# A fused attention and two-expert-layer kernel: Silu written into the product's PSUM bank, a new plan, three later loads

## The chip, the cores and the metric

One core of a Trainium2 chip runs the whole program once. The metric is the device time of one execution in microseconds (us), 815.83 us as the median of three executions of the kernel before (813.26 to 817.79). Engines are named as the profile names them: PE is TensorE (PEld its weight loads), DVE is VectorE, ACT is ScalarE, POOL is GpSimd, SP is SyncE, whose queue issues nearly all transfers.

## The reference

Three stages follow each other. An attention-like recurrence with a decaying state per head, over 4 batches, 8 heads, 768 steps and 48 features; a layer whose hidden value is the largest of three products; a gated layer with Silu.

```python
def _attn_ref(r, k, v, w, u):
    for t in range(S):
        cur = einsum('bhd,bhe->bhde', u * k[t], v[t])
        y[t] = einsum('bhd,bhde->bhe', r[t], state + cur)
        state = w[t][..., None] * state + einsum('bhd,bhe->bhde', k[t], v[t])

x = y as 3072 rows of 384
h = maximum(maximum(x @ w1, x @ w2), x @ w3)        # 768 wide
x = h @ w_out                                       # 384 wide
g = x @ w_gate                                      # 1536 wide
out = (g * (1 / (1 + exp(-g))) * (x @ w_val)) @ w_out2
```

## The kernel before

The tokens are cut into six blocks of 512. The first half of the run does the recurrence in 24 steps (six blocks of four head groups) and, as blocks get ready, the first layer: `up` (three products of each of six hidden tiles, whose maximum DVE takes in `up_out`) and `down`. Every fp32 operand is split into a high and a low part, and a product is three matmuls (`mm3`: high by high, high by low, low by high). `wload` brings the raw weights, DVE turns their words into fp32 (`bits`), ACT and DVE split them (`whigh`, `wlow`). `gather` copies 16 rows of one head group into the tiles of the others by DMA; the head group whose number is last in a block (the third row tile, k = 2) needs no gather in block 0, since PE puts its rows in place (`lend`). `up` of block 0 starts as soon as these parts are there.

The second half (from about 404 us) is the gated layer. It goes through three pairs of blocks (d = 0, 1, 2) and, for each, four units of weights, so twelve units n of about 33 us. A unit computes gate (v = 0) and value (v = 1) by a scheme of fewer products: fifteen operands made of sums of blocks (`y_sum` on POOL, split by `op_high` on ACT and `op_low` on DVE or POOL) are multiplied by fifteen sums of weights (`w_sum` on POOL, split by `w_high` on ACT and `w_low`), 45 matmuls per v in `product`. The partial sums in PSUM are taken out by ACT (`snap`, L978) or added by DVE (`join`, L983 and L985, one operand in PSUM and one in SBUF) and POOL (`mix`, L990 and L993, all in SBUF), which leaves six gate tiles and six value tiles in SBUF. For each of the six k, ACT then applies Silu in place in SBUF (`silu`, L997), DVE multiplies the two SBUF tiles into a PSUM bank (`times`, L1004), ACT copies that bank as the high part (`prod_high`, L1018) and DVE subtracts it for the low part (`prod_low`, L1021). Two PSUM banks serve the six products in turn, one named mm3 and one named pt, so the product of a k waits for `prod_low` of the second product before it. The order of k is PORDER = 5, 2, 1, 3, 0, 4. In the next unit, six projections (`proj`, nine matmuls each, the first three for c = 1, then three for c = 0) stand between the products at places that the table GAPS gives, and DVE adds them to the output (`collect`, L1046); one PSUM bank (po) serves most projections in turn.

Nothing in the program is ordered by hand. Plan.order places all instructions of all engines: each item has an engine, a cost, items it waits for and a due time, and due times are passed back to what comes before. At every step it looks at the items that could start within a window of the earliest start, and for each engine takes the smallest key, due + weight x start - a bonus for an item of the same kind as the last. Items marked port get longer when DVE and POOL both work on SBUF. The result is the program order of each engine, and engines run strictly in that order; only waits on data decide at run time. TUNE holds due times of groups (u0 and u1: the splitting of the weights of units 0 and 1; p0 to p3: the splitting of the projection weights; op: the operands of a new d; gaps: which row of GAPS a unit uses). The tiles raw0 and raw1 take turns for every large load of weight words, in a fixed list of turns (chunks): the words of unit 1, the last raw weights, the words of unit 0, then projection words of units 1 and 2, words of unit 2, projection words of unit 0, and so on. A load waits until the last user of its tile is done.

The rows of GAPS that the change speaks of; a key is (v, step after which the projection stands):

```python
# GAPS[0]
    {(0, 10): 0, (0, 13): 1, (1, 2): 2, (1, 6): 3, (1, 9): 4, (1, 12): 5},
# GAPS[1]
    {(0, 10): 0, (0, 13): 1, (1, 3): 2, (1, 8): 3, (1, 10): 4, (1, 12): 5},
# GAPS[2]
    {(0, 10): 0, (0, 13): 1, (1, 8): 2, (1, 9): 3, (1, 11): 4, (1, 13): 5},
# GAPS[6]
    {(0, 11): 0, (0, 14): 1, (1, 4): 2, (1, 7): 3, (1, 10): 4, (1, 12): 5},
```

Of the kernel before, what the change touches and what calls it, by code (L numbers as in the profile page):

```python
# [30 lines left out]
NPART = 5  # L31
W_LO, W_HI = 0.74, 1.35
TINY = 2.0 ** -14
TUNE = {'soon': 13.15, 'up5': -18.02, 'check': 23.6, 'bits': -8.01, 'u1': 339.54, 'u0': 393.49, 'prep': -25.06, 'xpre': 89.82, 'xgap': 8.15, 'xafter': 20.23, 't': -4.09, 'te': 2.32, 'p1': 405.42, 'p2': 412.78, 'p0': 6.62, 'p3': -14.49, 'slow': (3, 5, 6, 8, 10), 'op': -1.97, 'sums': -12, 'mix5': (0, 3), 'words2': -11.06, 'gaps': (1, 0, 3), 'collect': 1.99, 'v': 3.99}
GAPS = (
# [7 lines left out]
)  # L43

class Plan:  # L50
# [20 lines left out]
    def order(self):  # L71
# [27 lines left out]
        while avail:  # L99
            best = None  # L100
            for t in avail:
                at = max([free.get(t["eng"], 0.0), t["after"]] + [
                    d["end"] + d["lat"] + (t["slack"] if d["eng"] != t["eng"] else 0.0) for d in t["deps"]
                ])
                if t["slot"]:
                    o = held_by.get(count.get(t["slot"], 0) % t["slot"])
                    held = [r for r, part in o["readers"] if part in (None, 0)] if o else []
                    if any(r["start"] is None for r in held):
                        continue
                    at = max([at] + [r["end"] + 0.1 for r in held])  # L110
                t["at"] = at
                if best is None or at < best:
                    best = at
            first = {}
            for t in avail:
                if t.get("at") is not None and t["at"] <= best + 0.3:
                    k = first.get(t["eng"])
                    t["key"] = t["due"] + 15 * t["at"] - self.STAY * (t["kind"] == last.get(t["eng"]))
                    if k is None or t["key"] < k["key"]:
                        first[t["eng"]] = t  # L120
            for t in avail:
# [188 lines left out]
def fused(ctx: ExitStack, tc: tile.TileContext, pk, ub, wt_all, out):  # L310
# [439 lines left out]

    def up(c, f, m):
        ps = pss[c, f, m] = mm([128, NT], "ps")
        for k in range(3):
            mm3(ps, hi[f][:, 3 * m + k, :], lo[f][:, 3 * m + k, :], xh[c, k], xl[c, k], k == 0, k == 2)

    def up_out(c, f, m):
        if m == 0 and c == 0:
# [234 lines left out]
            b = buf[n, v, k]  # L992
            nc.gpsimd.tensor_tensor(b, b, buf[n, v, "u" if k == 3 else "d"], ALU.add)  # L993

    def silu(n, k):
        b = buf[n, 0, k]
        nc.scalar.activation(b, b, AF.Silu)  # L997

    gated = {}

    def times(n, k):
        e = PORDER.index(k) % 2
        gated[n, k] = (psO[0] if e else psM).tile([128, NT], F32, tag="pt" if e else "mm3", name="pt")
        nc.vector.tensor_tensor(gated[n, k], buf[n, 0, k], buf[n, 1, k], ALU.mult)  # L1004

    MIX5 = TUNE["mix5"]
    FINALS = (5, 2, 0, 1, 3, 4)
# [64 lines left out]

    p = Plan()

    SHARED = (y_sum, w_sum, op_low, w_low, mix, times, p_low, hidden, bits)

    def on(eng, cost, fn, *args):
        port = fn in SHARED and eng in ("DVE", "POOL")
# [6 lines left out]
            return t  # L1085
        return make

    UP0, PERIOD, LAST = 33.0, 62.0, 49.0
    START = [UP0 + (PERIOD * c + 6 if c else 0) for c in range(NC_)]
    SECOND = START[5] + LAST  # L1090

# [291 lines left out]
            L["chain"] = before  # L1383


    L["outer", 3]["deps"].append(L["take", 2])
    L["state0", 3]["deps"].append(L["lower", 2])
    L["suffix", 4]["deps"].append(L["state1", 3])
# [106 lines left out]
    def finish(n, k, j, due):  # L1495
        e = PORDER.index(k)
        by = AT_P[n, 0] - 4 + TUNE["te"] * e
        t = L["times", n, k] = on("DVE", 0.62, times, n, k)([j, L["silu", n, k]] + ([L["pl", *last_t[0]]] if len(last_t) > 1 else [L["y1d", 5, q] for q in range(3)]), by + TUNE["t"], slack=0.2)
        last_t[:] = last_t[-1:] + [(n, k)]
        if n == NU - 1:  # L1500
            war = [("x", n, 1, FINALS.index(k))]
        elif n:
            war = [("pj", n - 1, k % 2, 2)]
        else:
            war = [L["down", 5, 2, 1]] + (users[24] if k in (1, 3) else [L["wl", m, v, e] for m in STAGED for v in range(2) for e in range(3)] if k == 2 else [])
        h = on("ACT", 0.6, prod_high, n, k)([t], by - 2, slack=0.3)
        waits.append((h, war))
        slow = False
        L["pl", n, k] = on("POOL" if slow else "DVE", 1.35 if slow else 0.62, prod_low, n, k, nc.gpsimd if slow else nc.vector)([h], by - 1, slack=0.3)

    def buf_war(n, v, k):
        prev_ = (n, 0) if v else (n - 1, 1)
        first_ = [L["down", 5, 2, 1], close]
        if k == "u":
            return [L["mix", *prev_, 3], L["mix", *prev_, 5]] if prev_[0] >= 0 else first_
        if k == "d":
            return [L["mix", *prev_, 4], L["mix", *prev_, 5]] if prev_[0] >= 0 else first_
        pv = n - len(BUFS[v, k])
        if pv < 0:
            return first_  # L1520
        return [L["times", pv, k]]

    STEPS = (("s", 1), ("s", 0), ("s", "u"), ("j", "u"), ("s", 3), ("s", 4), ("s", "d"), ("s", 2), ("j", 2), ("j", 5),
             ("j", 2), ("j", 0), ("j", 1), ("j", 3), ("j", 4))
# [3 lines left out]
    def x_step(n, v, i, due):  # L1528
# [27 lines left out]
            L["mix", n, v, 4] = on("POOL", 1.35, mix, n, v, 4)([a, act[n, v, 5]], due + 4, slack=0.4)  # L1556
        if i in (9, 10, 11, 12, 13, 14):
            if v == 0:
                L["silu", n, k] = on("ACT", 0.6, silu, n, k)([a], due + SOON + 6, slack=0.5)
            else:  # L1560
                ready[k] = a
                if i == 14:
                    for q in PORDER:
                        finish(n, q, ready[q], due + SOON)
# [145 lines left out]
```

## Time and profile before

| what | value |
|---|---|
| device time, median of three (range) | 815.83 us (813.26 to 817.79) |
| the profiled execution's own time | 817.55 us |
| its span, first to last instruction | 815.8 us |
| PE busy | 788.6 us, 97% |
| DVE busy | 643.2 us, 79% |
| ACT busy | 458.2 us, 56% |
| POOL busy | 301.9 us, 37% |
[...]

The profile is of one execution. Busy shares are averages over stages with different limits; what a change is worth is read at the places where PE stands still, and there from what ended the wait.

### The profile page before, as it was taken

The numbers are of one execution on the slowest core, as the hardware profiler recorded it, in microseconds if no ns is written. First come the engines' busy times: TensorE is split into PE (matmuls) and PEld (weight loads), VectorE is DVE, ScalarE is ACT, GpSimd is POOL, SyncE is SP. The second block draws the span as 40 slices with busy tenths as digits, with TensorE's granted clock in tenths as the row PEclk, the third lists the DMA queues.
The fourth block names the chain that finished last, engine by engine and source line by source line (L and its number), as shares of the span: only waits on it lengthen the run. The fifth ranks groups of instructions, "written<-read, shape, count | busy, mean of one in ns | idle before, by whom it ended". The sixth has DMA issues, their size and how long they took to land.

```text
span 815.8 us, 15826 instructions
## 1 busy us (share of the span) xinstructions
PE 788.6 (97%) x6140; PEld 642.9 (79%) x6140; DVE 643.2 (79%) x930; ACT 458.2 (56%) x983; POOL 301.9 (37%) x281
## 2 busy tenths in 40 slices
PE   6999999999999999999999999999999999999997
PEld 5788668888888888888777887768888878888885
DVE  7889999977979967689758769796486787846864
ACT  5633564665454744445368655665864786666340
POOL 1000255221131010279848888533543262212210
PEclk9599999999999999999989999999999999999999
DMA  9745465774675752678683548678786776657202
GB/s 290 217 157 187 139 166 161 211 248 110 182 220 160 195 195 96 226 262 316 238 293 154 189 173 299 226 272 283 245 299 216 264 268 208 238 157 254 95 1 81
DMA packets 46482, 167.02 MB, mean 205 GB/s; under 512 B 6048, under 2 KB 11040, under 8 KB 41152
## 3 DMA queue, kind: packets, MB, share of 16 engines
q1 hardware_dynamic: 46256, 165.81, 62.2%
q8 instruction: 50, 0.82, 0.4%
q14 instruction: 32, 0.26, 0.1%
q10 hardware_dynamic: 144, 0.13, 0.1%
HBM read 123.84 MB, written 40.11 MB: 201 GB/s over the span
## 4 chain that ended last, share of the span: by engine, by line
PE 88%; DVE 6%; ACT 2%; issue 2%; DMA 1%; POOL 1%; SPq 0%; DVEq 0%; ACTq 0%; POOLq 0%
PE px L969 15%; PE py L969 13%; PE ps L660 10%; PE ps L662 10%; PE ps L661 10%; PE po L660 6%; PE po L662 6%; PE po L661 6%; PE y L550 2%; PE ps L781 2%; PE kp L524 2%; DVE W L933 2%; PE sc L606 2%; PE sc L510 1%; PE pa L481 1%
## 5 line engine op out<-in xcount | busy, mean ns | idle before, releaser
L969 PE MATMUL px<-yo,W 128*128 128x512 f32 x567 | 148.7, 394 | 5.8 <-ACT sb L978 3.1
L969 PE MATMUL py<-yo,W 128*128 128x512 f32 x498 | 132.1, 390 | 0.0
L969 PEld LDWEIGHTS px<-yo,W 128*128 128x128 f32 x567 | 107.5, 190 | 30.3 <-DVE sb L983 4.0
L993 POOL TENSOR_TENSOR sb<-sb 128x512 f32<-128x512 f32 x46 | 62.4, 1359 | 182.6 <-ACT sb L978 159.9
L660 PE MATMUL ps<-xh,hi 128*128 128x512 f32 x324 | 129.9, 401 | 0.0
L662 PE MATMUL ps<-xh,lo 128*128 128x512 f32 x324 | 127.2, 393 | 0.0
L661 PE MATMUL ps<-xl,hi 128*128 128x512 f32 x324 | 127.2, 393 | 0.0
L969 PEld LDWEIGHTS py<-yo,W 128*128 128x128 f32 x498 | 93.9, 189 | 19.6
L983 DVE TENSOR_TENSOR sb<-px,sb 128x512 f32<-128x512 f32 x95 | 64.2, 685 | 37.0 <-PE px L969 32.9
L660 PE MATMUL po<-pr,Wp 128*128 128x512 f32 x213 | 83.8, 393 | 3.0 <-DVE acc L1046 3.0
L661 PE MATMUL po<-pr,Wp 128*128 128x512 f32 x213 | 83.1, 390 | 1.3 <-DVE pr L1021 1.3
L662 PE MATMUL po<-pr,Wp 128*128 128x512 f32 x213 | 83.0, 390 | 0.0
L1018 ACT ACTIVATE pr<-pt 128x512 fp32r<-128x512 f32 x71 | 42.0, 599 | 61.2 <-DVE pt L1004 55.9
L978 ACT ACTIVATE sb<-px 128x512 f32<-128x512 f32 x96 | 56.5, 599 | 35.1 <-PE px L969 31.9
L662 PEld LDWEIGHTS ps<-xh,lo 128*128 128x128 f32 x324 | 61.4, 189 | 13.1
L660 PEld LDWEIGHTS ps<-xh,hi 128*128 128x128 f32 x324 | 61.6, 190 | 12.8 <-issue 0.2
L661 PEld LDWEIGHTS ps<-xl,hi 128*128 128x128 f32 x324 | 61.6, 190 | 12.3 <-issue 0.2
L424 POOL COPY total<-I 128x8 f32<-128x8 f32 x24 | 12.3, 514 | 156.3 <-DVE s L442 75.8
L1004 DVE TENSOR_TENSOR pt<-sb 128x512 f32<-128x512 f32 x71 | 63.5, 909 | 0.6
L764 DVE TENSOR_TENSOR hw<-hw,ps 128x512 f32<-128x512 f32 x60 | 40.7, 678 | 27.1 <-PE ps L662 11.8
L1046 DVE TENSOR_TENSOR acc<-po,acc 128x512 f32<-128x512 f32 x53 | 36.3, 686 | 29.1 <-PE po L662 28.8
L997 ACT ACTIVATE sb<-sb 128x512 f32<-128x512 f32 x72 | 44.6, 632 | 22.3 <-DVE sb L983 21.9
(188 smaller groups left out, 1584.2 us busy)
## 6 DMA issues: line engine op xcount, KB each, us to landing
W<-wsd SPq DMA_DIRECT2D x54, 640.0 KB, 5.1
raw<-wt SPq DMA_DIRECT2D x27, 1152.0 KB, 6.7
inpA<-pk SPq DMA_DIRECT2D x42, 294.0 KB, 5.4
Wp<-wpd SPq DMA_DIRECT2D x10, 1152.0 KB, 5.4
wsd<-W SPq DMA_DIRECT2D x17, 640.0 KB, 4.3
wfd<-fp32s SPq DMA_DIRECT2D x12, 576.0 KB, 4.7
inpT<-pk SPq DMA_DIRECT2D x16, 384.0 KB, 4.2
inpV<-pk SPq DMA_DIRECT2D x24, 200.0 KB, 4.2
```

Of the source, the lines that this page charges most:

```text
L660: nc.tensor.matmul(ps, lh, rh, start=first, stop=False)
L661: nc.tensor.matmul(ps, lh, rl, start=False, stop=False)
L662: nc.tensor.matmul(ps, ll, rh, start=False, stop=last)
L764: nc.vector.tensor_tensor(hws[f], hws[f], pss[c, f, m], ALU.max)
L969: nc.tensor.matmul(X[n, v, ch], w, x, start=first and k == 0, stop=k == 2, skip_group_check=True)
L978: nc.scalar.activation(sbuf(n, v, k), X[n, v, ch], AF.Copy)
L983: nc.vector.tensor_tensor(b, X[n, v, ch], b, ALU.add)
L993: nc.gpsimd.tensor_tensor(b, b, buf[n, v, "u" if k == 3 else "d"], ALU.add)
L997: nc.scalar.activation(b, b, AF.Silu)
L1004: nc.vector.tensor_tensor(gated[n, k], buf[n, 0, k], buf[n, 1, k], ALU.mult)
L1018: nc.scalar.activation(prod[n, k][:, 0, :], gated[n, k], AF.Copy)
L1046: nc.vector.tensor_tensor(acc[a], t, acc[a], ALU.add)
```

## The change

There are five edits. First, `silu` no longer works in place: it reads the gate tile in SBUF and writes its result into the PSUM bank that the product will use, and the multiplication (renamed `gate_times`, no longer marked port) reads that bank and the value tile in SBUF and writes the bank again. In the plan, a product's Silu therefore waits for the bank (for `prod_low` of the second product before it) as the multiplication did, and the gate tile is free again after Silu. Second, the tuned numbers are new, and the planner's weight, window and bonus become tuned numbers from 85 us of the plan on (29.41, 0.99 and 0.74, in place of 15, 0.3 and 2.0). Of the due times, u1 goes from 339.54 to 380, u0 from 393.49 to 370.17, p1 from 405.42 to 354.2, p2 from 412.78 to 397.32 and op from -1.97 to -11.67. Third, the projections use other rows of GAPS: row 6 in place of 1 for most units, row 2 in place of 0 for units 4 and 8; units 1 to 3 keep row 3. Fourth, the loads `wload` 2, `load_a` 6 and `load_v` 5 wait in the plan for the gather of head group 2 of block 0. Fifth, `up` of the first hidden tile of block 0 takes the row tiles in the order 2, 0, 1.

```diff
@@ -31,7 +31,13 @@
 NPART = 5
 W_LO, W_HI = 0.74, 1.35
 TINY = 2.0 ** -14
-TUNE = {'soon': 13.15, 'up5': -18.02, ..., 'u1': 339.54, 'u0': 393.49, ..., 't': -4.09, 'te': 2.32, 'p1': 405.42, 'p2': 412.78, 'p0': 6.62, 'p3': -14.49, ..., 'op': -1.97, ..., 'gaps': (1, 0, 3), ...}
+TUNE = {'wt': 29.41, 'win': 0.99, 'stay': 0.74, 'period': 62.0, 'soon': 14.07, 'up5': -17.12, ..., 'u1': 380, 'u0': 370.17, ..., 't': -8.63, 'te': 2.5, 'p1': 354.2, 'p2': 397.32, 'p0': 14.36, 'p3': -2.49, ..., 'op': -11.67, ..., 'gaps': (6, 2, 3), ...}
 GAPS = (
     {(0, 10): 0, (0, 13): 1, (1, 2): 2, (1, 6): 3, (1, 9): 4, (1, 12): 5},
     {(0, 10): 0, (0, 13): 1, (1, 3): 2, (1, 8): 3, (1, 10): 4, (1, 12): 5},
@@ -111,11 +113,12 @@
                 t["at"] = at
                 if best is None or at < best:
                     best = at
+            wt, win, stay = (TUNE["wt"], TUNE["win"], TUNE["stay"]) if best > 85.0 else (15.0, 0.3, 2.0)
             first = {}
             for t in avail:
-                if t.get("at") is not None and t["at"] <= best + 0.3:
+                if t.get("at") is not None and t["at"] <= best + win:
                     k = first.get(t["eng"])
-                    t["key"] = t["due"] + 15 * t["at"] - self.STAY * (t["kind"] == last.get(t["eng"]))
+                    t["key"] = t["due"] + wt * t["at"] - stay * (t["kind"] == last.get(t["eng"]))
                     if k is None or t["key"] < k["key"]:
                         first[t["eng"]] = t
             for t in avail:
@@ -750,8 +753,9 @@
     def up(c, f, m):
         ps = pss[c, f, m] = mm([128, NT], "ps")
-        for k in range(3):
-            mm3(ps, hi[f][:, 3 * m + k, :], lo[f][:, 3 * m + k, :], xh[c, k], xl[c, k], k == 0, k == 2)
+        turn = (2, 0, 1) if c == 0 and f == 0 else (0, 1, 2)
+        for e, k in enumerate(turn):
+            mm3(ps, hi[f][:, 3 * m + k, :], lo[f][:, 3 * m + k, :], xh[c, k], xl[c, k], e == 0, e == 2)
     def up_out(c, f, m):
         if m == 0 and c == 0:
@@ -992,16 +996,15 @@
             b = buf[n, v, k]
             nc.gpsimd.tensor_tensor(b, b, buf[n, v, "u" if k == 3 else "d"], ALU.add)
+    gated = {}
     def silu(n, k):
-        b = buf[n, 0, k]
-        nc.scalar.activation(b, b, AF.Silu)
-    gated = {}
-    def times(n, k):
         e = PORDER.index(k) % 2
         gated[n, k] = (psO[0] if e else psM).tile([128, NT], F32, tag="pt" if e else "mm3", name="pt")
-        nc.vector.tensor_tensor(gated[n, k], buf[n, 0, k], buf[n, 1, k], ALU.mult)
+        nc.scalar.activation(gated[n, k], buf[n, 0, k], AF.Silu)
+    def gate_times(n, k):
+        nc.vector.tensor_tensor(gated[n, k], gated[n, k], buf[n, 1, k], ALU.mult)
     MIX5 = TUNE["mix5"]
     FINALS = (5, 2, 0, 1, 3, 4)
@@ -1072,7 +1075,7 @@
     p = Plan()
-    SHARED = (y_sum, w_sum, op_low, w_low, mix, times, p_low, hidden, bits)
+    SHARED = (y_sum, w_sum, op_low, w_low, mix, p_low, hidden, bits)
     def on(eng, cost, fn, *args):
         port = fn in SHARED and eng in ("DVE", "POOL")
@@ -1085,7 +1088,7 @@
             return t
         return make
-    UP0, PERIOD, LAST = 33.0, 62.0, 49.0
+    UP0, PERIOD, LAST = 33.0, TUNE["period"], 49.0
     START = [UP0 + (PERIOD * c + 6 if c else 0) for c in range(NC_)]
     SECOND = START[5] + LAST
@@ -1383,6 +1386,8 @@
             L["chain"] = before
+    for key in (("wload", 2), ("la", 6), ("lv", 5)):
+        L[key]["deps"].append(L["gather", 2, 1])
     L["outer", 3]["deps"].append(L["take", 2])
     L["state0", 3]["deps"].append(L["lower", 2])
     L["suffix", 4]["deps"].append(L["state1", 3])
@@ -1495,7 +1500,9 @@
     def finish(n, k, j, due):
         e = PORDER.index(k)
         by = AT_P[n, 0] - 4 + TUNE["te"] * e
-        t = L["times", n, k] = on("DVE", 0.62, times, n, k)([j, L["silu", n, k]] + ([L["pl", *last_t[0]]] if len(last_t) > 1 else [L["y1d", 5, q] for q in range(3)]), by + TUNE["t"], slack=0.2)
+        free_ = [L["pl", *last_t[0]]] if len(last_t) > 1 else [L["y1d", 5, q] for q in range(3)]
+        g = L["silu", n, k] = on("ACT", 0.6, silu, n, k)([L["gate", n, k]] + free_, by + TUNE["t"] - 1, slack=0.3)
+        t = L["times", n, k] = on("DVE", 0.62, gate_times, n, k)([j, g], by + TUNE["t"], slack=0.2)
         last_t[:] = last_t[-1:] + [(n, k)]
         if n == NU - 1:
             war = [("x", n, 1, FINALS.index(k))]
@@ -1518,7 +1525,7 @@
         pv = n - len(BUFS[v, k])
         if pv < 0:
             return first_
-        return [L["times", pv, k]]
+        return [L["times" if v else "silu", pv, k]]
     STEPS = (("s", 1), ("s", 0), ("s", "u"), ("j", "u"), ("s", 3), ("s", 4), ("s", "d"), ("s", 2), ("j", 2), ("j", 5),
              ("j", 2), ("j", 0), ("j", 1), ("j", 3), ("j", 4))
@@ -1556,7 +1563,7 @@
             L["mix", n, v, 4] = on("POOL", 1.35, mix, n, v, 4)([a, act[n, v, 5]], due + 4, slack=0.4)
         if i in (9, 10, 11, 12, 13, 14):
             if v == 0:
-                L["silu", n, k] = on("ACT", 0.6, silu, n, k)([a], due + SOON + 6, slack=0.5)
+                L["gate", n, k] = a
             else:
                 ready[k] = a
                 if i == 14:
```

## Rows read from the trace of the kernel before

**Rows 1.** The page: busy us, share, instructions; PE clock in 40 slices.

```profile
PE 788.6 (97%) x6140; PEld 642.9 (79%) x6140; DVE 643.2 (79%) x930; ACT 458.2 (56%) x983; POOL 301.9 (37%) x281
...
PEclk9599999999999999999989999999999999999999
```

**Rows 2.** PE's waits after 390 us: total, times, longest.

```profile
PE px L969 <- ACT sb L978: 3.1, 1, 3.1
PE po L660 <- DVE acc L1046: 3.0, 3, 1.4
PE px L969 <- DVE sb L983: 2.5, 3, 1.3
PE po L661 <- DVE pr L1021: 1.3, 1, 1.3
```

**Rows 3.** The same from 50 to 390 us, the longest.

```profile
PE sc L606 <- issue: 0.6, 1, 0.6
```

**Rows 4.** One stretch: us, PE, PEld, DVE, ACT, POOL busy (instructions), PEclk, DMA, GB/s.

```profile
405.00:410.00 5.00, 1.85 (x9) 1.24 (x7) 0.00 (x0) 1.85 (x3) 0.89 (x2) 0.87 1.03 389
```

**Rows 5.** Timeline around that stretch: start, length, engine, line [idle before].

```profile
400.61 0.53 SPq L877 DMA_DIRECT2D wq<-wfd  x1
...
408.15 1.16 ACT L944 ACTIVATE Wp<-wq 128x1152 fp32r<-128x1152 f32 x1 [4.21 <-DMA wq<-wfd]
```

**Rows 6.** The chain that ended last, just after it: start, length, what.

```profile
409.85 2.93 PE px L969 x6
...
416.20 1.36 PE py L969 x6
```

**Rows 7.** The page's group of the multiplication: busy, mean ns | idle before.

```profile
L1004 DVE TENSOR_TENSOR pt<-sb 128x512 f32<-128x512 f32 x71 | 63.5, 909 | 0.6
```

**Rows 8.** Single lines of the program: ns of one, min/median/max, first and last start.

```profile
L1004 DVE TENSOR_TENSOR pt<-sb x71: 682/693/2584, 428.8 to 799.3; 128x512 f32<-128x512 f32 x71
...
L983 DVE TENSOR_TENSOR sb<-px,sb x95: 673/691/692, 411.6 to 790.2; 128x512 f32<-128x512 f32 x95
...
L997 ACT ACTIVATE sb<-sb x72: 618/632/660, 413.5 to 781.9; 128x512 f32<-128x512 f32 x72
```

**Rows 9.** Timeline: long multiplications and the PE stops after them.

```profile
430.16 2.58 DVE L1004 TENSOR_TENSOR pt<-sb 128x512 f32<-128x512 f32 x1
...
435.98 0.97 PE L969 MATMUL px<-yo,W 128*128 128x512 f32 x3 [0.74 <-DVE sb L983]
...
498.42 1.73 DVE L1004 TENSOR_TENSOR pt<-sb 128x512 f32<-128x512 f32 x1
...
503.80 0.96 PE L969 MATMUL px<-yo,W 128*128 128x512 f32 x3 [1.33 <-DVE sb L983]
```

**Rows 10.** Timeline at the change from d = 0 to d = 1.

```profile
520.40 3.34 DVE L868 TENSOR_TENSOR yo<-xr,yo 128x512 fp32r<-128x512 f32 x2
...
524.39 0.50 PE L660 MATMUL po<-pr,Wp 128*128 128x512 f32 x1 [1.24 <-DVE acc L1046]
...
537.08 1.36 DVE L1004 TENSOR_TENSOR pt<-sb 128x512 f32<-128x512 f32 x1
...
541.39 0.50 PE L661 MATMUL po<-pr,Wp 128*128 128x512 f32 x1 [1.34 <-DVE pr L1021]
```

**Rows 11.** Timeline at the end of the last unit.

```profile
797.54 0.68 DVE L1021 TENSOR_TENSOR pr<-pt,pr 128x512 fp32r<-128x512 f32 x1
...
798.64 0.39 PE L662 MATMUL po<-pr,Wp 128*128 128x512 f32 x1
```

**Rows 12.** Timeline at the first `up`, and gathers before it.

```profile
33.76 1.17 SPq L654 DMA_DIRECT2D xl<-xsl  x2
...
38.26 0.60 ACT L645 ACTIVATE xl<-y 128x512 fp32r<-128x512 f32 x1 [0.89 <-PE y L636]
...
38.45 0.63 PE L661 MATMUL ps<-xl,hi 128*128 128x512 f32 x1
...
45.59 0.75 DVE L166 TENSOR_SCALAR tmp<-raw 128x1152 int32<-128x1152 int32 x1
```

More of the change, by code (lines that the diff above doesn't have):

```diff
@@ L33 @@
 TINY = 2.0 ** -14
-TUNE = {'soon': 13.15, 'up5': -18.02, 'check': 23.6, 'bits': -8.01, 'u1': 339.54, 'u0': 393.49, 'prep': -25.06, 'xpre': 89.82, 'xgap': 8.15, 'xafter': 20.23, 't': -4.09, 'te': 2.32, 'p1': 405.42, 'p2': 412.78, 'p0': 6.62, 'p3': -14.49, 'slow': (3, 5, 6, 8, 10), 'op': -1.97, 'sums': -12, 'mix5': (0, 3), 'words2': -11.06, 'gaps': (1, 0, 3), 'collect': 1.99, 'v': 3.99}
+TUNE = {'wt': 29.41, 'win': 0.99, 'stay': 0.74, 'period': 62.0, 'soon': 14.07, 'up5': -17.12, 'check': 29.53, 'bits': -7.63, 'u1': 380, 'u0': 370.17, 'prep': -36.51, 'xpre': 82.52, 'xgap': 7.97, 'xafter': 11.7, 't': -8.63, 'te': 2.5, 'p1': 354.2, 'p2': 397.32, 'p0': 14.36, 'p3': -2.49, 'slow': (3, 5, 6, 8, 10), 'op': -11.67, 'sums': -9.09, 'mix5': (0, 3), 'words2': 0.75, 'gaps': (6, 2, 3), 'collect': 6.42, 'v': 2.26}
 GAPS = (
```

## The prediction

> **What bounds the kernel now.** I read the page's busy line and its clock row first: PE works 788.6 of 815.8 us, and no other engine passes 79% [rows 1]. The change adds and removes no matmul, so time can come only from the 27.2 us in which PE stands still and from stretches at half clock. Some of that is out of reach: before the first data, after the last matmul, and the cold clock of the second slice, while the first blocks pass engine by engine. PE's waits after 390 us, the second view, add up to 9.9 us: 3.1 behind ACT, 3.0 behind `collect`, 2.5 behind `join`, 1.3 behind `prod_low` [rows 2]. Between 50 and 390 us the longest wait is 0.6 us, so that long stretch is already full [rows 3]. Then I looked at what stood before each wait, by windows and timeline.
>
> The 3.1 us lie at the start of the second half. Between 405 and 410 us PE works 1.85 of 5.00 us and DVE none, while the DMA engines are fully busy [rows 4]. ACT has stood 4.21 us before the splitting of a projection weight, whose load went out at 400.61 and ended its wait at 408.15 [rows 5]; the snaps that PE needs are behind it in ACT's queue. [...] The other waits are all behind DVE, which is late for a moment.
>
> **The change part by part.** I work against the profiled execution: its own time is 817.55 us, 1.75 us more than the span and 1.7 us over the median. I carry the sum over to the median of 815.83.
>
> *The multiplication.* Its 71 like calls take 909 ns in the mean [rows 7], 682 at the least and 2584 at the most; `join`, with one operand in PSUM, stays between 673 and 692 in all 95 [rows 8]. Both run beside POOL, so the stretched ones are those with two SBUF operands. The new form has one in PSUM, so I give it 0.685 us: 72 x (0.909 - 0.685) = 16 us less of DVE. Most of that was idle time anyway; it counts where PE waited behind DVE. The 2.58 us call at 430.16 is 1.9 too long, and the PE wait of 0.74 at 435.98 goes; the 1.73 us call at 498.42 is 1.05 too long, and of the 1.33 at 503.80 about 0.3 is left [rows 9]. Sum -1.8 us. The third of the `join` waits, 2.5 - 0.74 - 1.33 = 0.4 us, is too small to argue about; bounds -2.5 to 0.
>
> [...]
>
> *Silu in the bank.* No Silu is added: 72 of 0.632 us on ACT [rows 8], which has room. No row shows ACT from SBUF into PSUM; the nearest are Silu itself, and I keep 0.63 (bounds 0.58 to 0.70: on ACT this is 4 us in 400 at most). What is new is where Silu stands. Before, it was done as soon as its gate tile was there. Now four of a unit's six must wait until `prod_low` of the second product before has freed the bank, and the chain of one bank becomes Silu, multiplication, high part, low part. That adds 0.63 plus two hand-offs, say 0.1, so 0.73 us per turn where the chain is late. Behind a waiting Silu in ACT's queue stand the snaps, and PE waits for those after few products; behind a waiting multiplication on DVE stand the joins. In a quiet unit the cover is the distance from the last join to the first projection in the next unit, ten products of 0.68 us, some 6.8 us [rows 6], against two turns of 2 x 0.63 + 2 x 0.685 + hand-offs, about 5.6. So it is covered, by 1 us or so. At the two changes of d it isn't: the wait of 1.34 at 541.39 is for `prod_low`, after a multiplication of 1.36 us that loses 0.67 and a Silu that brings 0.73 [rows 10], so this wait stays. I take 2 x 0.73 = +1.5 us there; bounds 0 and, if each of eleven units paid two turns, 11 x 1.46 = +16.
>
> At the very end cover is thin but there: the low part read at 798.64 is done at 797.54 + 0.68 = 798.22 [rows 11], 0.42 us ahead. PE is busy with the last projections of the unit before, so I take 0; if Silu came fully on top, it is 0.73 - 0.42 = 0.3.
>
> *The start of the second half.* The load of rows 5 takes its turn on a raw tile after the weight words of unit 0; they get a due time 23 us earlier (u0), the splitting of the projection weight one 15 us earlier (p2), that of unit 1 one 51 us earlier (p1). If unit 0 is split sooner, the load goes out sooner and ACT doesn't stand. The price is order on POOL and DVE, which then do the operands later. Bounds -6.05 (all gone) and 0 (the same wait, elsewhere). I take -6.05: 7.5 us of load time [rows 5] have to be found, and u0 alone moves by 23.
>
> *The operands of a new d.* `op_low` on DVE beside POOL's takes 3.34 us for two, and `collect` behind it holds PE 1.24 us at 524.39 [rows 10]; three such waits make 3.0 [rows 2]. This pair has only SBUF operands and stays slow. A due time 9.7 us earlier and later projections in units 4 and 8 may part them; the tile is freed only by the last unit of the old d, which limits that. Bounds -3.0 and +1.5; I take half, -1.5.
>
> *New order of the first layer.* From 85 us of the plan all is sorted anew, over a stretch with hardly a wait [rows 3]. It can gain 1 us and lose more; I take +0.5 (bounds -1 to +3).
>
> *Held loads and the order 2, 0, 1.* In block 0 the second matmul of `up` ran at 38.45, and the low part of row tile 2 is ready at 38.26 + 0.60 = 38.86 [rows 12]. With tile 2 first, that matmul waits 0.45 us, and no gather is waited for in either order. The three loads now queue on SP behind the gather that ends its issue at 33.76 + 1.17 = 34.9; the words of `wload` 2 are read at 45.59 [rows 12], 10.7 us later, and the slow load above took 7.5. Nothing on PE waits. +0.45 (bounds 0 to +1; the clock is low there, and a later rise could add).
>
> Sum: -1.8 + 1.5 - 6.05 - 1.5 + 0.5 + 0.45 = -6.9 us. The profiled execution would become 817.55 - 6.9 = 810.65, the median 815.83 - 6.9 = 808.9 us.
>
> **The rivals.** *A: the load wait stays.* The DMA engines are full around 405 us [rows 4], and a plan that was right about its load would not have let ACT stand there in the first place. Then only -0.85 is left: 815.0. Against it: u0 moves by three times the length of the load. *B: Silu at the head of ACT's queue, slower.* If the banks aren't free when the plan thinks, each unit pays turns of the chain: 11 units x 1.46 = 16.1 us in place of the 1.5, so 808.9 + 14.6 = 823.5. It decides from 0.63 + 0.1 = 0.73 us per unit on: 11 x 0.73 = 8.0 eats the rest (-8.4), and the kernel is no faster. For it: the spare of a quiet unit is 1 us by my count, and ACT is shared with the snaps. Against: the plan knows the bank and its release. *C: nearly all waits go.* Taking the best bounds, -6.05 - 2.5 - 3.0 - 1.0 gives 803.3. Against: no plan meets every load and every stretched operation. *D: the multiplication is stretched still,* since something other than the operand sets it; then -1.8 falls away, 810.7. The 95 joins speak against it [rows 8]. *E: a new stop in the reordered part that drops the clock.* One place like that of rows 4 to 6 costs 6.05; two of them against the sum give 808.9 + 12.1 = 821.
>
> **How the numbers follow.** The forecast (with D) 0.48, for 805 to 811.7; C 0.08; A, or the forecast with one new stop of 3 to 6 us, 0.27; B 0.10; E 0.07. A measurement of this kernel tells 0.5%, some 4 us, from no change. Faster (under 811.7) is the forecast and C, 0.56; the same 0.27; slower (over 819.9) B and E, 0.17. The predicted time is 808.9. Leaving out half of C below and the slower cases above, the range is 803.5 to 818.
>
> **What would show it.** The multiplication near 690 ns throughout; no ACT wait of 3 us and no drop of the clock around 400 to 415 us; the waits behind `join` under 1 us together; those behind `prod_low` not under 1.3 but not over 4. Wrong if PE's waits behind ACT snaps or `prod_low` return in every unit (B), if the load wait is back with its clock drop (A, E), or if the stretch from 85 to 390 us shows waits of over 2 us.

## The result and the profile after

The changed kernel takes 807.83 us in the median (805.78 to 809.09), the kernel before, run beside it, 816.81 (813.26 to 819.31). The ratio is 0.989 [0.985, 0.994]: it is faster, by some 1%, and the forecast of 808.9 lies 1 us off. A second set, experiment e5, gives 809.53 (807.82 to 811.11) and a ratio of 0.991 [0.988, 0.994]. The sum came out right; several of its terms did not, as the experiments show, and that they cancelled is in part luck.

The page of the changed kernel, to be held against [rows 1]: busy us and share of the span (804.0 us), and the clock in 40 slices.

```profile
PE 783.2 (97%) x6140; PEld 638.1 (79%) x6140; DVE 624.0 (78%) x930; ACT 451.4 (56%) x983; POOL 286.1 (36%) x281
...
PEclk9999999999999999999999999999999999999999
```

PE is busy 5.4 us less for the same matmuls: the half clock of [rows 6] is gone, and in this execution the clock also rose earlier in the first 50 us (its first record, at full, is at 31 us; before, it rose at 44). (The second slice of the clock row is not what it seems; see the last section.) DVE is busy 19.2 us less. PE's waits from 395 us on, the answer to [rows 2] (total, times, longest):

```profile
PE py L973 <- ACT y1s L793: 1.0, 1, 1.0
PE po L664 <- DVE pr L1024: 0.4, 2, 0.2
PE py L973 <- ACT sb L982: 0.4, 1, 0.4
PE px L973 <- DVE sb L987: 0.3, 1, 0.3
PE po L663 <- DVE acc L1049: 0.2, 1, 0.2
```

They add up to 2.3 us, from 9.9. Behind DVE there were 6.8 (3.0 + 2.5 + 1.3), now there are 0.9. Lines L1004 (Silu) and L1007 (the multiplication) of the changed kernel (ns of one, min/median/max), against [rows 8]:

```profile
L1004 ACT ACTIVATE pt<-sb x72: 585/602/651, 411.0 to 785.8; 128x512 f32<-128x512 f32 x72
...
L1007 DVE TENSOR_TENSOR pt<-pt,sb x71: 683/690/700, 423.3 to 786.9; 128x512 f32<-128x512 f32 x71
```

The multiplication is never over 700 ns, where its longest had been 2584. Silu into PSUM takes 602, inside the bounds of 580 to 700 that I had set from Silu in SBUF.

The start of the second half, against [rows 4, 5]: two windows (us, PE, PEld, DVE, ACT and POOL busy with instructions, clock, DMA share, GB/s), then the timeline.

```profile
400.00:405.00 5.00, 3.99 (x18) 2.99 (x17) 1.46 (x2) 3.59 (x7) 5.00 (x5) 1.00 0.88 281
405.00:410.00 5.00, 4.67 (x21) 3.56 (x20) 3.44 (x5) 2.40 (x5) 4.53 (x3) 1.00 0.70 226
```

```profile
399.76 1.52 PE L973 MATMUL px<-yo,tu 128*128 128x512 f32 x6
...
401.27 1.17 ACT L948 ACTIVATE Wp<-wq 128x1152 fp32r<-128x1152 f32 x1 [1.13 <-DMA wq<-wfd]
...
402.98 0.96 PE L973 MATMUL py<-yo,tu 128*128 128x512 f32 x3 [1.01 <-ACT y1s L793]
```

The projection weight is split at 401.27 instead of 408.15, and ACT stands 1.13 us for its load instead of 4.21. PE pays 1.01 us, as a `down_out` is behind that splitting in ACT's queue. PE then works 4.67 of the 5 us from 405 on (1.85 before), at the full clock.

For the comparisons below I split the profiled runs at the first `px` matmul of the second half (401.10 us before, 399.76 after) and take the rest of the span as the second half. That is 815.8 - 401.1 = 414.7 us before and 804.0 - 399.8 = 404.2 after: 10.5 us less, of which the waits are 9.9 - 2.3 = 7.6 and the half clock of [rows 6] 2.95: from 409.85 to 416.20 us fifteen matmuls took 6.35 us, where fifteen at the rate of the six right after them (1.36 us) take 3.4. A window of the kernel before has the granted clock there, 0.50, third from the end:

```profile
409.00:414.00 5.00, 4.15 (x10) 3.28 (x11) 2.19 (x3) 4.00 (x7) 4.13 (x3) 0.50 0.74 261
```

The first half has no large part in the gain: from the first `down` of block 0 (91.96 before, 90.73 after) to the second half it is 309.1 and 309.0 us. The two profiled executions stand 0.7 us above and 2.0 us below their medians, so the medians differ by less (9.0, and 6.9 in the second set) than these profiles do (11.8). Of the 11.8, 1.2 us lie before the first `down`, where the clock rose earlier; no edit is shown to bring that.

### The profile page after: what moved, and what is told of

Same layout as the page of the kernel before. It is cut to its first block, busy times and chain, and to the rows that moved or that the text cites. A ratio compares the mean times of both kernels' runs of the same rounds, so it can differ in the third digit from the quotient of the medians.

```text
span 804.0 us, 15834 instructions
## 1 busy us (share of the span) xinstructions
PE 783.2 (97%) x6140; PEld 638.1 (79%) x6140; DVE 624.0 (78%) x930; ACT 451.4 (56%) x983; POOL 286.1 (36%) x281
## 4 chain that ended last, share of the span: by engine, by line
PE 88%; DVE 6%; issue 2%; POOL 1%; ACT 1%; DMA 1%; DVEq 0%; ACTq 0%
PE px L973 14%; PE py L973 13%; PE ps L663 11%; PE ps L664 10%; PE ps L665 10%; PE po L663 6%; PE po L664 6%; PE po L665 6%; PE y L553 2%; PE ps L785 2%; PE kp L527 2%; PE sc L609 2%; PE sc L513 1%; PE pa L484 1%; PE y L566 1%
## 5 line engine op out<-in xcount | busy, mean ns | idle before, releaser
L973 PE MATMUL py<-yo,W 128*128 128x512 f32 x498 | 130.4, 389 | 0.4 <-ACT sb L982 0.4
L1004 ACT ACTIVATE pt<-sb 128x512 f32<-128x512 f32 x72 | 42.6, 603 | 27.4 <-DVE pr L1024 27.3
L989 DVE TENSOR_TENSOR sb<-sb,py 128x512 f32<-128x512 f32 x47 | 32.2, 685 | 28.3 <-ACT sb L982 25.0
```

The source lines that it names most:

```text
L973: nc.tensor.matmul(X[n, v, ch], w, x, start=first and k == 0, stop=k == 2, skip_group_check=True)
L989: nc.vector.tensor_tensor(b, b, X[n, v, ch], ALU.subtract)
L1004: nc.scalar.activation(gated[n, k], buf[n, 0, k], AF.Silu)
```

## The experiments

Each median is compared with runs of the kernel before on the same chip: 815.76 us (31 runs) for e1 to e4, 816.43 (18) for e5 to e8, 815.96 (16) for e9 to e12. The second half is that of the one profiled execution of each; for the changed kernel two executions give 404.2 and 404.1. The profiled executions of e2 and e9 lie 3.2 and 2.9 us below their medians and that of e11 5.5 above. Where two runs of different groups are compared below, the times are taken as they stand; the kernel before differs by up to 1.1 us between the groups.

| kernel | median us | ratio [95%] | second half us |
|---|---|---|---|
| before | 816.81 | 1 | 414.7 |
| changed | 807.83 | 0.989 [0.985, 0.994] | 404.2 |
| e1 changed, Silu and multiplication on SBUF operands | 816.15 | 1.001 [0.999, 1.002] | 412.2 |
| e2 before, with the new Silu alone | 813.12 | 0.997 [0.995, 0.999] | 409.1 |
| e3 changed, planned for the old Silu | 815.02 | 0.999 [0.996, 1.001] | 411.4 |
| e4 before, with the six weight due times alone | 813.87 | 0.997 [0.995, 0.999] | 409.9 |
| e5 changed, again | 809.53 | 0.991 [0.988, 0.994] | 404.1 |
| e6 changed, without the two early edits | 809.09 | 0.989 [0.985, 0.993] | 405.4 |
| e7 changed, Silu in two steps | 808.72 | 0.992 [0.989, 0.995] | 406.3 |
| e8 changed, old weight due times | 821.1 | 1.005 [1.002, 1.007] | 418.6 |
| e9 before, with the new Silu and the due times | 810.09 | 0.993 [0.990, 0.995] | 406.1 |
| e10 changed, old due time of the operands | 805.89 | 0.989 [0.986, 0.992] | 403.2 |
| e11 changed, old gaps | 806.71 | 0.989 [0.986, 0.992] | 402.1 |
| e12 changed, old sorting | 814.07 | 0.997 [0.995, 0.998] | 410.9 |

### e1: the operands alone, in the same order

```diff
     def silu(n, k):
+        b = buf[n, 0, k]
-        nc.scalar.activation(gated[n, k], buf[n, 0, k], AF.Silu)
+        nc.scalar.activation(b, b, AF.Silu)
...
     def gate_times(n, k):
...
-        nc.vector.tensor_tensor(gated[n, k], gated[n, k], buf[n, 1, k], ALU.mult)
+        nc.vector.tensor_tensor(gated[n, k], buf[n, 0, k], buf[n, 1, k], ALU.mult)
```

> The changed kernel with its instruction order on all engines, but with Silu in place in SBUF and the multiplication of two SBUF tiles into the bank, as before. Nothing else differs, so the difference to the changed kernel is the operands alone. Theory 1 (the form takes away only the waits behind visibly stretched multiplications, the rest is the order): 1.8 us slower than the changed kernel, some 809.6. Theory 2 (all of PE's waits behind DVE, 6.8 us before and 1.3 us after, went with the stretched multiplications): 5 us or more slower, 813, and the waits behind join and collect are back. Theory 3 (the order alone did it): no difference, 807.8, with the multiplications long again but nobody waiting for them.

It took 816.15 us: with the same program order on every engine (the two traces have it so), two SBUF operands lose the whole gain, and the price of 1.8 us that my sum gave them falls. Against the changed kernel that is 8.3 us (first set) or 6.6 (e5), in the second half 412.2 - 404.1 = 8.1. PE's waits in the second half, the first three, and the multiplication in the view by lines (busy us, mean ns | idle before it):

```profile
PE po L664 <- DVE pr L1025: 3.0, 4, 1.7
PE po L663 <- DVE acc L1050: 1.9, 5, 0.7
PE px L973 <- DVE sb L987: 1.1, 1, 1.1
```

```profile
L1008 DVE TENSOR_TENSOR pt<-sb 128x512 f32<-128x512 f32 x71 | 60.0, 868 | 1.9 <-ACT sb L1003 1.7
```

The waits behind DVE are 6.0 us instead of 0.9. Two more things differ from the changed kernel: the gate tile stays in use until the multiplication, and Silu no longer waits for the bank. Neither shows as a cause in e1's trace: no `snap` waits behind the multiplication, and the 27.3 us that ACT waits before Silu in the changed kernel turn into waits for the multiplication before `prod_high`, 84.8 us against 58.0.

One place shows how a stretched call grows on its way. This is e1 at the change from d = 0 to d = 1: two multiplications beside POOL, the low part behind them, the stop, and then the chain of work that ended last.

```profile
530.71 2.88 DVE L1008 TENSOR_TENSOR pt<-sb 128x512 f32<-128x512 f32 x2
...
531.31 1.73 POOL L994 TENSOR_TENSOR sb<-sb 128x512 f32<-128x512 f32 x1
...
534.84 0.50 PE L664 MATMUL po<-pr,Wp 128*128 128x512 f32 x1 [1.75 <-DVE pr L1025]
```

```profile
536.80 2.56 PE px L973 x6
539.36 1.05 PE py L973 x3
```

The same place in the changed kernel:

```profile
527.99 1.28 DVE L1007 TENSOR_TENSOR pt<-pt,sb 128x512 f32<-128x512 f32 x2
...
528.72 1.30 POOL L994 TENSOR_TENSOR sb<-sb 128x512 f32<-128x512 f32 x1
...
530.52 0.50 PE L664 MATMUL po<-pr,Wp 128*128 128x512 f32 x1 [0.20 <-DVE pr L1024]
```

The two multiplications take 1.60 us longer, PE stands 1.75 us instead of 0.20, and nine matmuls shortly after it take 2.56 + 1.05 = 3.61 us, where nine at the full clock take 2.04 (1.36 for six, [rows 6]). So 1.6 us on DVE cost about 3.1 on PE. The granted clock is 0.66 in the window from 535 to 540 us. This is the only half clock in e1's second half up to the last matmul, 1.6 of the 8.1 us; nearly all the rest are stops like this one. From one matmul's start to the next, stops and slow matmuls add up to 13.5 us in e1's second half and to 5.6 in that of the changed kernel. POOL's operation, too, is 0.43 us shorter beside the form with the PSUM operand (1.30 against 1.73).

### e2, e4 and e9: Silu alone, due times alone, both

e2 puts the new `silu`, `gate_times`, their waits and the shorter SHARED list into the kernel before, with all numbers old. e4 changes six numbers of the kernel before and nothing else. e9 does both.

```diff
-..., 'u1': 339.54, 'u0': 393.49, ..., 'p1': 405.42, 'p2': 412.78, 'p0': 6.62, 'p3': -14.49, ...
+..., 'u1': 380, 'u0': 370.17, ..., 'p1': 354.2, 'p2': 397.32, 'p0': 14.36, 'p3': -2.49, ...
```

> The kernel before with the new Silu and multiplication alone; the old due times, weights, gaps and early part, planned again with these operations. Theory 1: -1.8 + 1.5 = -0.3 us against the kernel before, the load wait of 3.1 us with its half clock still there. Theory 2: -5.5 us, 811. Theory 3: no change. Rival B (Silu at the head of ACT's queue): over 4 us slower than before, with PE waits behind ACT snaps or behind the low part in many units.

> The kernel before with only the six due times of the weight splitting changed (u0, u1, p0 to p3). By the prediction's term for the start of the second half: the 4.2 us stop of ACT and the half clock go, -6.05 us, some 810. By rival A (the DMA engines are full there, the wait stays): within 1 us of the kernel before. In between: the wait goes but another one comes in the same stretch.

> The kernel before with the new Silu and multiplication and the six new due times of the weight splitting, nothing else. Each alone gave -2.6 and -1.9 us. If the parts add up: -4.5 us, 811.5. If the one opens what the other gains (with the old form the due times traded the ACT stop for waits behind stretched operations on DVE): -6 to -8 us, 808 to 810, near the changed kernel.

Against 815.76, e2 is 2.6 us faster, and e4 1.9. Each leaves something standing. The largest waits of PE in the second half, e2 first, then e4:

```profile
PE px L969 <- ACT sb L978: 2.7, 1, 2.7
PE po L660 <- DVE acc L1045: 1.9, 2, 1.4
```

```profile
PE px L969 <- DVE sb L983: 5.7, 5, 2.0
PE po L660 <- DVE acc L1046: 1.2, 2, 0.7
...
PE px L969 <- ACT sb L978: 0.6, 1, 0.6
```

In e2 the stop behind ACT is still there, but in this execution no half clock follows it (the six matmuls after it take 1.65 us, and the granted clock is 1.00 from 405 to 425 us), so its second half of 409.1 shows more gain, 5.6 us, than the medians do. In e4 it is down from 3.1 to 0.6 us, but the waits behind `join` went from 2.5 to 5.7. The longest, in e4's timeline, is behind a `join` that itself stood 1.84 us for POOL's `mix`:

```profile
455.06 0.69 DVE L983 TENSOR_TENSOR sb<-px,sb 128x512 f32<-128x512 f32 x1 [1.84 <-POOL sb L990]
...
455.80 0.96 PE L969 MATMUL px<-yo,W 128*128 128x512 f32 x3 [2.03 <-DVE sb L983]
```

So with the weights taken earlier POOL and DVE are late with the sums. e9 gains 815.96 - 810.09 = 5.9 us, more than 2.6 + 1.9 = 4.5; what PE waits there behind `join` is 1.2 us:

```profile
PE po L661 <- DVE pr L1020: 1.6, 3, 0.8
PE px L969 <- DVE sb L983: 1.2, 2, 1.1
...
PE po L660 <- DVE acc L1045: 0.5, 1, 0.5
```

The earlier splitting seems to pay fully only with the new Silu beside it. That 5.9 exceeds 4.5 by more than chance is not certain: the two intervals of e2 and e4 are each some 3.5 us wide. As measured, e9, with the old sorting, gaps and first edits of block 0 and every other number old, already has 5.9 of the 6.9 to 9.0 us: everything else that is new adds only 1 to 3.

### e3: the new numbers with the old Silu

e3 is the changed kernel, early edits included, with `silu`, `times`, their waits and the SHARED list of the kernel before; the plan is made anew for them.

> The changed kernel's due times, weights, gaps and early edits, planned again with the old Silu and the old multiplication. If the numbers carry the gain whatever the form is, it comes within 2 us of the changed kernel (808 to 810); if the numbers fit only the new form, the waits behind DVE come back: 812 to 816.

It took 815.02 us, 0.7 less than the kernel before, which can't be told from nothing. The three longest waits are the old ones behind DVE:

```profile
PE px L973 <- DVE sb L987: 2.1, 2, 1.6
PE po L663 <- DVE acc L1050: 2.1, 2, 1.5
PE py L973 <- DVE sb L989: 1.7, 1, 1.7
```

The form of the multiplication is thus worth 2.6 us in the old plan (e2), 3.8 with the six due times (813.87 - 810.09) and 5.5 to 7.2 with all new numbers (815.02 less 809.53 or 807.83). The plan is worth 0.7 without the form and 3.6 to 5.3 with it.

### e5 and e6: the changed kernel again, and without the two early edits

e5 is the changed kernel. e6 takes out the three held loads and the order 2, 0, 1:

```diff
-        turn = (2, 0, 1) if c == 0 and f == 0 else (0, 1, 2)
+        turn = (0, 1, 2)
...
-    for key in (("wload", 2), ("la", 6), ("lv", 5)):
-        L[key]["deps"].append(L["gather", 2, 1])
```

> The changed kernel once more, with more executions, to see how its first 50 us come out. [...] If the clock there is a matter of chance in every kernel, as in the kernel before and in the experiments so far (some executions at 0.998, most at 0.98 to 0.99), most executions lie lower, and the median comes out 1 to 2 us higher.

> The changed kernel without its two early edits: the three loads are not held back, and the first up takes the row tiles in the order 0, 1, 2. By the prediction's terms (0.46 us of waiting for the low part of row tile 2, the loads hidden): 0.5 us faster than the changed kernel in the first 50 us, the rest the same within 2 us since the plan is made again. If the early edits matter for the clock: 1 to 3 us slower, with a lower mean clock.

They took 809.53 and 809.09 us. The early edits bring nothing that can be measured. The wait that I had put on PE for them at 0.45 us is there, 0.46 in the timeline of the changed kernel, but `down` begins no later for it: at 90.73 and 91.37 us with the edits, at 91.73 without, and at 91.72 in e1, which has the edits and a clock that rose about as late as in e6 (0.83 in the window from 40 to 45 us, 0.68 in e6).

```profile
37.39 0.50 PE L664 MATMUL ps<-xl,hi 128*128 128x512 f32 x1 [0.46 <-ACT xl L648]
```

### e7: Silu made twice as long

```diff
-        nc.scalar.activation(gated[n, k], buf[n, 0, k], AF.Silu)
+        nc.scalar.activation(gated[n, k], buf[n, 0, k], AF.Copy)
+        nc.scalar.activation(gated[n, k], gated[n, k], AF.Silu)
```

> The changed kernel with Silu as two instructions in its place: a copy of the gate tile into the bank, and Silu in place in the bank, 0.6 us more in each turn of a bank and 43 us more of ACT; the order is otherwise that of the changed kernel. If the spare of a quiet unit is about 1 us for two turns, as the prediction counted, 1.2 us more is just over it: 0.2 us and up in eleven units, 2 to 6 us slower. If there is far more spare: within 1.5 us. If there is none (rival B's premise): 11 x 1.2 = 13 us slower.

It took 808.72 us, between the two sets of the changed kernel, although every turn of a bank is one operation longer (the line of e7 shows its second step; the first, a copy, has a median of 597 ns):

```profile
L1005 ACT ACTIVATE pt<-pt x72: 582/582/582, 411.0 to 789.2; 128x512 f32<-128x512 f32 x72
```

Yet the second half of its profile is 2.1 us longer than that of the changed kernel (406.3), so some cost is likely that the medians don't tell from the spread. It is not rival B's: 0.6 us in two turns of each of eleven units would be 13 us, and PE's waits behind `prod_low` are 0.4 us as in the changed kernel. DVE does stand behind Silu's second step, 8.1 us in 15 places (1.6 in three places before), and hardly any of it reaches PE. So the chain Silu, multiplication, high part, low part has far more room than the 1 us of my count. The page of the changed kernel, not of e7, has the wait that rival B feared (busy us, mean ns | idle before it): ACT stands 27.3 us before Silu for `prod_low`. And its timeline shows in a quiet unit why the first two products of a unit are not late for it: their two Silus are done, and their two multiplications come 9 us later. (The later four are closer: 0.2 us in one case of that unit.)

```profile
L1004 ACT ACTIVATE pt<-sb 128x512 f32<-128x512 f32 x72 | 42.6, 603 | 27.4 <-DVE pr L1024 27.3
```

```profile
602.44 0.60 ACT L1004 ACTIVATE pt<-sb 128x512 f32<-128x512 f32 x1 [2.43 <-DVE pr L1024]
...
605.68 0.60 ACT L1004 ACTIVATE pt<-sb 128x512 f32<-128x512 f32 x1
...
615.26 1.29 DVE L1007 TENSOR_TENSOR pt<-pt,sb 128x512 f32<-128x512 f32 x2
```

### e8: the old weight due times in the changed kernel

The edit is the six numbers of e4, the other way round, in the changed kernel.

> The changed kernel with the six old due times of the weight splitting (u0, u1, p0 to p3), the reverse of the experiment with those alone. If they take away the stop at the start of the second half, it comes back: an ACT stop of about 4 us at 405 with PE at half clock after it, 5 to 6 us slower. If the rest of the new plan avoids it, within 1.5 us.

It took 821.1 us, 11.6 more than e5 and slower than the kernel before. There is a stop at the start of the second half again. From the timeline: a store, the splitting on ACT that waits for it, and PE behind that; then two of PE's longest waits of the second half.

```profile
402.24 0.57 SPq L955 DMA_DIRECT2D wpd<-tup  x1
...
413.59 1.16 ACT L948 ACTIVATE Wp<-wq 128x1152 fp32r<-128x1152 f32 x1 [7.56 <-DMA wpd<-tup]
...
415.29 1.83 PE L973 MATMUL px<-yo,W 128*128 128x512 f32 x6 [2.42 <-ACT sb L982]
```

```profile
PE po L665 <- POOL Wp L952: 3.8, 1, 3.8
...
PE po L663 <- DMA Wp<-wpd: 2.2, 1, 2.2
```

ACT stands 7.56 us before the same line of the program, but not for the load of before: the wait ends with the store of the projection weight split before it, which went out at 402.24 (at 377.01 in the kernel before, at 369.60 in the changed one). And the larger part is new: in three places (1.0, 3.8 and 2.2 us) PE waits for a projection weight itself, which in the kernel before it never did. So the due times decide when the projection weights are ready, and with the other new numbers the old ones are worse than in the kernel before. Which of the six does it was not tried.

### e10, e11 and e12: the operands' due time, the gaps, the sorting

Each sets one group of numbers of the changed kernel back:

```diff
e10  -'op': -11.67
     +'op': -1.97
e11  -'gaps': (6, 2, 3)
     +'gaps': (1, 0, 3)
e12  -'wt': 29.41, 'win': 0.99, 'stay': 0.74
     +'wt': 15.0, 'win': 0.3, 'stay': 2.0
```

> The changed kernel with the old due time of the operands of a new d (op -1.97 in place of -11.67). By the prediction's term: the waits behind collect at the changes of d come back, 1.5 us slower than the changed kernel (809.5 in its second set of executions), at most 3. If the new form alone relieved DVE there: within 0.7 us.

> The changed kernel with the old places of the projections (rows 1 and 0 of the table in place of 6 and 2). If the places matter, 1 to 3 us slower with waits behind the low part or collect in many units; if not, within 0.7 us.

> The changed kernel with the planner's old weight, window and bonus (15, 0.3 and 2.0) everywhere. The prediction gave the new sorting +0.5 us in the first layer and counted nothing of it in the second half. By that: 0.5 us faster. If the plan is a fit of all numbers together: 2 to 6 us slower, with waits in the second half.

e10 and e11 took 805.89 and 806.71 us: neither number is worth anything, and both second halves are a little shorter, though the intervals overlap those of the changed kernel. (The profiled execution of e11 came to the second half late, at 408.3 us, after one stop of 3.0 us in the first half that the other kernels don't show at that length.) e12 took 814.07 us: without the new sorting 4.5 to 6.2 us are lost, and most of what the two profiles differ by lies in the second half (410.9 against 404.1). That is not what the sorting is worth by itself: e9 has the old sorting too, and 5.9 of the 6.9 to 9.0 us; it is the other new numbers that need the new sorting. The timeline shows one place: three splittings on DVE, with POOL splitting at the same time, ahead of a low part that PE waits for.

```profile
432.53 1.20 DVE L937 TENSOR_TENSOR W<-ww,W 128x256 fp32r<-128x256 f32 x2
432.68 1.36 POOL L937 TENSOR_TENSOR W<-ww,W 128x256 fp32r<-128x256 f32 x2
433.65 0.67 DVE L937 TENSOR_TENSOR W<-st,W 128x256 fp32r<-128x256 f32 x1
...
434.24 1.27 DVE L1024 TENSOR_TENSOR pr<-pt,pr 128x512 fp32r<-128x512 f32 x2
...
434.98 0.50 PE L664 MATMUL po<-pr,Wp 128*128 128x512 f32 x1 [2.16 <-DVE pr L1024]
```

After that stop PE's next matmuls run at half clock (three take 1.49 us at 436.92, where three took 0.86 at 431.03; the window from 435 to 440 us has a granted clock of 0.66). The old numbers give a bonus of 2.0 for staying with the same kind of item and look only 0.3 us ahead, which fits three splittings in a row; which of the three numbers does it was not tried.

## Why the prediction was right, step by step

**Start of the second half, -6.05.** The 6.05 is what the trace of before shows: the wait of 3.1 us and the 2.95 that the half clock after it cost. Right in place and mechanism: in the profile the stop went from 3.1 to 1.0 us and the half clock after it is gone, 2.1 + 2.95 = 5.05 us, and in e4 the due times alone bring it to 0.6, without half clock. The 2.95 is not fixed, though: in e2 no half clock followed a stop of 2.67 us at this place. What the step left out is the condition: in the old plan the same six numbers gain only 1.9 us (e4), since other work becomes late. I had named that price ("POOL and DVE, which then do the operands later") and counted it at nothing.

**The multiplication, -1.8 (bounds -2.5 to 0).** The mechanism was right, the size was the largest miss: 6.6 to 8.3 us by e1, outside the bounds. I had added up the PE stops behind two long calls in the order of before. That order was made by a planner that had these items marked as long, which may have kept them off PE's path. At most that is the smaller part: e3, planned anew for the long form, still stands 5.5 to 7.2 us behind the changed kernel, some 1 us less than e1. In the changed order a stretched call holds up `collect`, `join` and `prod_low` behind it (6.0 us of waits against 0.9), and one stop of PE there has half clock after it (1.6 us), which I had counted only at the load. Measured with the old numbers (e2), the whole edit gains 2.6 us, where my two terms for it came to 0.3.

**Silu in the bank, +1.5.** Wrong: no wait that it would explain is seen. Waits behind `prod_low` are 0.4 us, where I had given "not under 1.3" as a sign, and one more operation of 582 ns in every turn costs at most some 2 us in the whole half (e7); no run has Silu's new place alone. My count of a quiet unit set the whole chain of two turns against one distance of ten products; in the timeline beside e7 the Silus of two products stand 9 us ahead of their multiplications. Rival B (823.5) falls with it.

**Operands of a new d, -1.5.** The wait behind `collect` went from 3.0 to 0.2 us, more than the half that I took, but not by the due time and the gaps that I named: without either the waits stay away (e10, e11). They are back with two SBUF operands (1.9 us in e1, 2.1 in e3) and with the old sorting in the new plan (1.9 in e12), but e9, with the old sorting, has 0.5, and e2, with the new form and all old numbers, 1.9. So the freed DVE seems to be a condition and is not enough; what else it takes depends on the rest of the plan and stays open. Single calls of `op_low` are still stretched, to 2.4 us at the most in the second half.

**New order of the first layer, +0.5.** For the first layer the size is right: nothing to be seen, 309.1 and 309.0 us. But the step saw the new sorting only there. In the second half undoing it costs 4.5 to 6.2 us (e12), and I had no term for it; with the other numbers old, as in e9, it isn't needed for 5.9 us of the gain.

**Held loads and the order 2, 0, 1, +0.45.** The wait is there with 0.46 us (the rows of before gave 38.86 - 38.45 = 0.41); in the end nothing (e6).

That the sum came so near is luck in part. The gains are no separate ones: form and due times alone give 2.6 and 1.9 us, both together 5.9, the whole change 7 to 9. In the changed plan most of it is lost when any one of form, due times or sorting is taken out (6.6 to 8.3, 11.6, 4.5 to 6.2); these losses add up to far more than the gain, so they are not what each part is worth. A sum of terms, each costed in the kernel before, can't show that, and here what it had too small and what it counted without its condition happened to cancel.

Of the rivals, A's time (815.0) is near that of e1, e3 and e12, but for other reasons; in the change the load wait fell to 1.13 us on ACT. C named nearly all waits gone, and in the second half they are (2.3 of 9.9 us left); 803.3 was not reached. D is excluded by 700 ns at the most, and E's new stop with half clock is not seen: from 50 us to the last matmuls the clock is full (1.00 in the windows from 50 to 795 us). The multiplication's median is 690 ns with one PSUM operand (the changed kernel) and 693 with two SBUF operands (e1).

## What to carry to other kernels

The waits behind an operation that gets slow beside another engine show its cost in one order of the work only. Here they gave 1.8 us in the old order, and undoing the change in the new order, with that order held fixed, cost 6.6 to 8.3. Parts of such a change are tried in pairs, not only alone or by undoing: the due times gave 1.9 us alone, 3.0 with the new form (813.12 - 810.09), and the kernel loses 11.6 without them. Undoing a part of a plan whose numbers were fitted together shows what that plan rests on, not what the part is worth. Price a stop of PE at what follows it, too: 1.75 us of waiting cost 3.3 with the half clock after it.

## What was not expected of the hardware

The clock in the first 50 us differs between executions of one and the same kernel. Two windows of the changed kernel, first its first profile, then e5: full clock in the one, 0.78 in the mean in the other.

```profile
35.00:40.00 5.00, 3.83 (x46) 2.93 (x40) 5.00 (x7) 1.62 (x3) 1.09 (x1) 1.00 0.70 214
```

```profile
35.00:40.00 5.00, 3.83 (x36) 2.77 (x27) 5.00 (x7) 1.56 (x4) 1.17 (x1) 0.78 0.61 207
```

In e1, with the same order, it is 0.50 there. It is worth about 1 us in this order (first `down` at 90.73, 91.37 and 91.72 us), which is a part of the spread of every kernel here, and it comes with no edit.

A clock of 1.00 at the very start of a page can mislead. The changed kernel's page has it from the first slice, but its trace holds no record of the clock before 31 us, and PE's eight like matmuls take twice as long at 26 us as at 41 (a window, then the timeline):

```profile
25.00:30.00 5.00, 5.00 (x89) 4.53 (x92) 2.74 (x6) 3.26 (x13) 0.00 (x0) 1.00 0.81 171
```

```profile
26.09 1.86 PE L484 MATMUL pa<-inpA,rk 128*128 128x2 f32 x8
...
41.38 0.95 PE L484 MATMUL pa<-inpA,rk 128*128 128x2 f32 x8
```

In the kernel before, whose window from 25 to 30 us has 0.50, the like eight take 1.87 us at 25.56, and 0.95 at 44.72, after its clock rose. So the changed kernel is not shown at the full clock from 20 us on, as its row of the clock has it: in its first profile the clock stood at full from 31 us, where in e1 and in the kernel before it rose at 42 and 44. The mean granted clock of an execution is to be read with the same care.

Nor does half clock always follow a stop: it did after 1.75 us in e1 and 2.16 in e12 (0.66 in the window after each), it did not after 2.67 in e2 and 2.03 in e4 (1.00 from 405 to 425 and from 450 to 470 us). What decides it is open.
